# Turning three pairs of heads on TensorE, the second head's maxima row too, and a new table of the order

## The chip, the core and the metric

The kernel runs on one core of a Trainium2 chip. The metric is the device time of one execution in microseconds (us). The engines are named as the profile names them: PE (TensorE, matmul), DVE (VectorE), ACT (ScalarE), POOL (GpSimd) and SP (SyncE, which issues all DMAs of this kernel). PEld is PE's loading of weights, SPq is SP at issuing a DMA. Each engine works through its own instructions in the order in which they were written down; semaphores make it wait for others.

## The reference

An attention with pooled queries, then a mixer. Shapes: 4 batches, 8 heads, 1152 keys, 576 pooled queries, head width 64; 32 heads in all.

```python
def _attn_ref(q, k, v):
    q_pool = q.reshape(B, H, S // 2, 2, D).mean(axis=3)
    scores = scale * np.matmul(q_pool, k.transpose(0, 1, 3, 2))
    scores = scores - np.max(scores, axis=-1, keepdims=True)
    attn = np.exp(scores)
    attn = attn / (np.sum(attn, axis=-1, keepdims=True) + 1e-09)
    return np.matmul(attn, v)

def _moe_ref(x, w_tok1, w_tok2, w_ch1, w_ch2):     # x: (4, 576, 512)
    xt = x.transpose(0, 2, 1)
    u = x + (np.maximum(xt @ w_tok1, 0.0) @ w_tok2).transpose(0, 2, 1)
    return u + np.maximum(u @ w_ch1, 0.0) @ w_ch2
```

The weights arrive as 64-bit floats and are narrowed on the chip from their words.

## The kernel before, in words

**Numbers in two parts.** Each 32-bit operand of an important product is split into a high part, which PE takes in one pass, and a low part, what is left. A product is then two or three matmuls. For the scores a head has stacked operands: `KK` holds the keys' high part above their low part, `QQ` the queries' high part twice, and `K2`, `Q2` hold the rest of the product in 64 partitions. Partition 64 of `K2` is a row of -1, and partition 64 of `Q2` is the row of the queries' maxima, so that the score matmul itself subtracts the maximum (`scores` in `main`, L930 to L939: first `s<-qq,kk`, then `s<-q,k`). The row is needed before the second half of a head's first score.

**Heads come in pairs** (p = 0 to 15). `load_kq` (L665) loads keys and queries of two heads. For pair 0 the loads are wide: keys lie as they are in memory (`load_k`), queries with both members of a pool next to each other (`load_q`). PE turns these 128x128 blocks (`keys` L718, `queries` L747, steps L724 and L755). For all other pairs the loads are in blocks (`load_k_blocks` L674, `load_q_blocks` L680: twelve DMAs of runs of 128 bytes), laid so that DVE's transpose of 32x32 blocks completes the turn (L732, L764). The pooling addition is in `prep_kq` (L713 for pair 0, L707 for the others). ACT copies the high part out of PSUM, DVE subtracts it for the low part. `qd` holds the last 64 queries of both heads on a diagonal; ACT fills it for pair 0 (L778), two DMAs for the others (L782).

**`stack`** (L805) copies the parts by six DMAs per head into `QQ`, `KK`, `K2`, `Q2`.

**`maxima`** (L825) makes the raw scores of the high parts on PE (L871) and DVE reduces them (L873). From head 1 on, DVE reduces the three thirds of a query's keys to one column of `MH` (L838, L842), and four or five DMAs of single words turn the columns into the row of `Q2` (L846, L849). Head 0 goes another way (`first_maxima`, L882): DVE reduces into columns of `M0` (L893), PE turns them (L899), ACT copies the row (L906); the last 64 queries of head 1 come along there (L910).

**`main`** (L916) runs nine steps per head: scores of two key blocks, two exponentials on ACT (`pf` L951 in full, `ph` L954 the high part), their difference `pl` (L958; on POOL for the first four heads, on POOL or DVE after them), and the products with `v` (L985). **`finish`** (L1002) turns the result, forms denominators (L1041, L1044) and multiplies five blocks by the reciprocal on ACT (L1051). After each fourth head `token_mix` (L1055) mixes half of a batch over the tokens, with weights that `tok_weights` (L594) narrows early: ACT L638, POOL L640, DVE L644 to L655, ACT L653. Behind all heads the channel mixing runs (`mm3` L1214, `mm4` L1242).

**The order.** Nothing is issued as it is called. Each `step` adds an entry with an engine, an estimated cost and a due time (from the table `DUE`) to a plan, with its dependencies. `Plan.run` (L334) then issues them in an order that is read from the string `ORDER`, and gives the steps whose numbers stand in `OTHER` their second engine (`both` steps: POOL or DVE). Costs and due times served to make that table; `run` does not look at them:

```python
        near = np.frombuffer(zlib.decompress(base64.b85decode(ORDER)), np.uint8).reshape(2, -1)
        order = [self.steps[n] for n in np.cumsum(near.T.copy().view("<i2")[:, 0])]
        for n in OTHER:
            self.steps[n].eng, self.steps[n].cost = self.steps[n].other
```

Of the kernel before, what the change touches and what calls it, by code (L numbers as in the profile page):

```python
# [17 lines left out]
AF = mybir.ActivationFunctionType  # L18
# [19 lines left out]
    "scores": -2.93,  # L38
    "p_lo": 3.58,
    "sum": -9.57,  # L40
    "pv": 2.54,
    "o": -51.33,
    "finish": 8.58,
    "max": -33.49,
    "max_each": 0.15,
    "prep": -34.13,
    "v": 1.91,
    "stack": -25.67,
    "stack_2": -1.62,
    "mix": 3.46,  # L50
    "mix_x": 6.67,
    "w_tok": 25.38,
    "w_tok_each": 0.19,
    "w_bits": -16.65,
    "sum_each": 1.34,
    "pv_lo": -1.1,
    "lo_first": 24.87,
    "max_first": -16.17,
    "max_second": 26.42,
    "scores_each": -4.16,  # L60
    "p_hi": -0.36,
    "pv_one": -0.26,
    "finish_each": -13.78,
    "den_sum": -50.17,
    "x_lo": -20.89,
    "x": 46.21,
    "den": -101.88,
    "rd": -11.49,
    "u": 17.31,
    "u_each": -154.37,  # L70
    "max_of": -3.2,
    "max_row": -26.25,
    "max_first_each": -13.9,
    "q_pool": -8.21,
    "q_turn": 4.59,
    "k_each": 1.41,
    "k_hi": -501.55,
    "k_turn": -4.76,
    "q_diag": 2.44,
    "load_v_0": -10.17,  # L80
    "v_0": 20.76,
    "max_1": 24.7,
    "ut_load": 42.06,
    "k_lo": 1.85,
    "q_hi": -23.02,
    "q_lo": -22.23,
    "load_kq": -79.9,
    "load_v": -9.0,
    "v_lo": -23.38,
    "load_w_tok": -22.82,  # L90
    "mix_x_lo": -125.66,
    "mix_1": 1.01,
    "mix_t": -1.26,
    "mix_2": 3.21,
    "mix_u": -46.13,
    "w_ch": 7.79,
    "w_ch_each": 1.93,
    "ut_0": 13.85,
    "ut_1": -24.13,
# [7 lines left out]
class Due(dict):  # L107
# [16 lines left out]
    "TtF2szpK5X*m|`w4P8#;LPmT96=P&cKO6MnZeXr@N8hq0EUHY1D-5R|vDxAJ0&r<Nu9jSSJb-cvoP3M=#L%Kiiyku_o*8!!^bl&E79bf8tzc"
    "jtpuiR$8G$IbgcQ4mEe2|`;3=ajvl*yqdk4+KAi)y04jGo*4&rUrsOB%i6^z;iM=F-"
    "jK8$%N2f@@XF;ui@cTJ!gZgzTMc16r*Che43Y$HDRC;e%;2>iF1_L7jyv2cCF#$h%$^#IguGwMo^VxOFD=tyFxOTroMNbpzheMg0p*yZ|FNS"
    "XbH2TqTZ<Y&&a1+-"
    "e~aAG~Ajo>5NGF*`P_GaaOOqTDD*pIftSJwQ_f!?s=UH&Slx@YUY?KvYwkQxhvc7S+W!?{#?7GZjUx!Xx)#1VE>`w0mA_Yv%AqVj;<donByP"
    "4t94s`NJh&x_y(>cItAwrRhL9cB@j-wb=EgN1a6c>S5n*&-"
    "fvegT2lw;GML?ord@>eeXK>eb1y)JA>lZ^J85dZp}z;_sgoeD)dRg(i<htKJ_y7gQ0h7X6z159r7G}GidEmP$TaEzquC)QIW}jymH$?cZb{q"  # L130
    "KI;0yL!+)?m(Qhy`1ppFE2Lwl;g|C(3G5ucY2%y)p4qaR+#UGD5wo#X)72u^3+dC(`ShysynZJ6YpHiC@K5UU*}|sX_pNARD85GcM$+R$n|B"
    "qDhWB|R>3(5cPUniGkgWXhB$MG6dwyynIy{d1m9#!@QDiT0BjG{2tj}{!D$QqoHvN-"
    "j;76#9Ob(*3*21&@)5}v7cc$DJojkcZXYx@~Wk8n3aOmB!7ggfg>C!XCud$s+&<`>l8tC+MSKIQCgk{*QHf;^2-"
    "J5afXUBmltAAn^HCKG^iYLYzSt@In{UXp4&L8HTH~Y|cbgH;}hJTw)J$s~tAMQXJHg?kPu<@sjoStKc-"
    "k)?V=Ev_Eev}V_%01Wlrhy4LjV8Xg#(K>F>fqyW^wUbirobfgI_q+1+M{5=jY_MavYSKOH;7Jy;g6e)>gOL<toWTKQ4TBE8e)Ld^Y#H<QPOy"
    "$L;F|7d^&2pVRdZTd!LA)22lq*Mzp-jGLDBgMqyPZxgN7FBrL(uoTBQ@lh5MOW30?2HD9E6(D_GD&`aomA)hwKC?Cvz*Q>1km9cNTVp}E(AE"
    "B=D+*O|oUH<n*X7#qVOa8>K?Ji8owL+~PyRYA~H2lD5MW$$R`>PK&Ke991yWz8KMe?G=sPdieqo69U-"
    "^tF|+hvt|Kxf}Z{Lq$78+2P6gb}FpN>SwPD$#^3J)3W~Q$?rtNO2k&wqcjRrgn{3thrbrU$z!MFn9Q^&Tsd~UiQHo4dCwA##?wt!osF!8rQ;"
    "Z_Z&+dfVy0$QvJ`pIIoXzMn=V@x#Ok#e}5_MwJXhkf7A8HaG&M)8ue}T)1m-x_aA~OH<~O5s-"
    "7r6bg!74^4s3*y?D}L2U*`^Zl7mgt)G<Rx2JP;z!}?;g}Ie#t5K(?ob1vx?5Gr<nN?~zPF;U({xOReQOAikQ_j?fC5+DpqxVS_Xxr#7QERFz"  # L140
    "WY1&Zra&i{((_!*+3BePQ&tttyd)aCChnTe2Qwe|?%W&~m>N**a(l!Vb;oZVz(M0)jxfXanI-NVnK4zjYi0C$z7kCha4odmH#`(SHSc*%;;I"
# [36 lines left out]
    "$_0i8_I<z|Hcpsx;Y{xRRrP1buMsAX={GdHs4L#L(NcD;ce+i*DEy7HlxKapcIhi;T$wfESk!a#R%L%23_m^UYoF4$#%<4bQJO^K_1&TJZSN"
# [1174 lines left out]
```

## Time and profile before

| what | value |
|---|---|
| time, median of 3 runs | 893.98 us (892.14 to 895.11) |
| the profiled execution | 896.53 us, of it span 894.8 us |
| mean granted clock of PE | 0.981 of 2.4 GHz |
| PE busy | 850.1 us (95%), 5322 matmuls |
| PEld, DVE, ACT, POOL busy | 785.5, 625.6, 551.7, 478.0 us |
| attention and token mixing | up to about 580 us |
| channel mixing | about 580 us to the end |

How to read it: the profile is one execution. Busy times are unions of an engine's instructions. The records of matmuls overlap, so a busy PE need not be at its peak; the spacing of matmuls tells its pace. Waits are put down to what came last before an instruction began, by the events that the profile holds.

### The profile page before, as it was taken

The numbers are of one execution on the slowest core, as the hardware profiler recorded it, in microseconds if no ns is written. First come the engines' busy times: TensorE is split into PE (matmuls) and PEld (weight loads), VectorE is DVE, ScalarE is ACT, GpSimd is POOL, SyncE is SP. The second block draws the span as 40 slices with busy tenths as digits, with TensorE's granted clock in tenths as the row PEclk, the third lists the DMA queues.
The fourth block names the chain that finished last, engine by engine and source line by source line (L and its number), as shares of the span: only waits on it lengthen the run. The fifth ranks groups of instructions, "written<-read, shape, count | busy, mean of one in ns | idle before, by whom it ended". The sixth has DMA issues, their size and how long they took to land.

```text
span 894.8 us, 15517 instructions
## 1 busy us (share of the span) xinstructions
PE 850.1 (95%) x5322; PEld 785.5 (88%) x5322; DVE 625.6 (70%) x1244; ACT 551.7 (62%) x1141; POOL 478.0 (53%) x378
## 2 busy tenths in 40 slices
PE   7659989999999999999999999999999999999998
PEld 5549879999988899998999999999998999989897
DVE  5767989999999898988998988788774323121202
ACT  4758889798899689898799898843431211111110
POOL 2868978898997769788688777423210000000000
PEclk9959999999999999999999999999999999999999
DMA  7997786786796677687765563256533301000101
GB/s 172 150 192 149 140 151 115 141 167 123 137 177 113 128 148 134 134 174 145 135 139 114 110 135 89 68 154 170 141 97 70 71 7 41 1 30 1 46 2 36
DMA packets 262207, 99.46 MB, mean 111 GB/s; under 512 B 233264, under 2 KB 245424, under 8 KB 262128
## 3 DMA queue, kind: packets, MB, share of 16 engines
q1 hardware_dynamic: 262128, 98.47, 54.2%
q8 instruction: 42, 0.69, 0.3%
q14 instruction: 37, 0.30, 0.1%
HBM read 46.40 MB, written 9.44 MB: 62 GB/s over the span
## 4 chain that ended last, share of the span: by engine, by line
PE 70%; DVE 10%; DMA 6%; ACT 6%; SPq 5%; issue 2%; POOL 1%; DVEq 0%; ACTq 0%; POOLq 0%
PE r L1214 16%; PE o L985 13%; PE s L1242 12%; PE s L937 12%; PE r L871 6%; PE o L1242 4%; DVE sum L965 3%; DVE mx L873 3%; PE r L1100 2%; ACT ph L954 2%; ACT pf L951 2%; DMA vn<-in_v_dram 2%; PE r L1082 2%; SPq L682 2%; DMA q<-mh 2%
## 5 line engine op out<-in xcount | busy, mean ns | idle before, releaser
L958 POOL TENSOR_TENSOR pl<-pf,ph 128x576 fp32r<-128x576 f32 x247 | 355.4, 1461 | 80.2 <-ACT ph L954 24.9
L873 DVE TENSOR_REDUCE mx<-r 128x1 f32<-128x384 f32 x384 | 192.4, 548 | 27.2 <-PE r L871 24.1
L985 PE MATMUL o<-ph,vv 128*128 128x288 f32 (+2 forms) x882 | 205.8, 300 | 2.2 <-DVE ot L998 1.0
L951 ACT ACTIVATE pf<-s 128x576 f32<-128x576 f32 x288 | 191.4, 684 | 21.6 <-PE s L937 19.3
L954 ACT ACTIVATE ph<-s 128x576 fp32r<-128x576 f32 x288 | 187.8, 661 | 27.1 <-PE o L985 12.7
L937 PE MATMUL s<-qq,kk 128*128 128x288 f32 x574 | 175.1, 313 | 10.0 <-ACT ph L954 6.8
L937 PE MATMUL s<-q,k 65*128 65x288 f32 x576 | 169.7, 302 | 13.5 <-DMA qn<-in_q_dram 10.9
L985 PE MATMUL o<-pl,vv 128*65 128x288 f32 (+1 forms) x576 | 149.3, 300 | 0.3 <-POOL pl L958 0.3
L1222 DVE SCALAR_TENSOR_TENSOR h<-r,h 128x384 fp32r<-128x384 f32 x72 | 39.2, 554 | 156.3 <-ACT h L1220 156.2
L1220 ACT ACTIVATE h<-r 128x384 fp32r<-128x384 f32 x72 | 34.9, 491 | 182.5 <-PE r L1214 182.4
L985 PEld LDWEIGHTS o<-ph,vv 128*128 128x128 f32 (+2 forms) x882 | 128.9, 153 | 8.8 <-DVE ot L998 3.2
L937 PEld LDWEIGHTS s<-qq,kk 128*128 128x128 f32 x574 | 110.7, 193 | 20.5 <-ACT ph L954 11.3
L871 PE MATMUL r<-kk,qq 128*128 128x384 f32 x372 | 123.9, 349 | 3.5 <-DMA qq<-qh 1.9
L1242 PE MATMUL s<-w,h 128*128 128x512 f32 x468 | 124.7, 394 | 1.1 <-DVE raw L1256 1.1
L937 PEld LDWEIGHTS s<-q,k 65*128 65x128 f32 x576 | 111.3, 193 | 14.4 <-DMA qq<-qh 11.1
L1214 PE MATMUL r<-big,w 128*128 128x384 f32 x576 | 113.1, 337 | 0.6 <-DVE h L1222 0.4
L1214 PEld LDWEIGHTS r<-big,w 128*128 128x128 f32 x576 | 102.4, 188 | 6.7 <-DVE h L1222 0.6
L965 DVE TENSOR_REDUCE sum<-pf 128x96 f32<-128x960 f32 x90 | 100.7, 1133 | 0.6 <-ACT pf L951 0.6
L1242 PEld LDWEIGHTS s<-w,h 128*128 128x128 f32 x468 | 86.7, 188 | 15.2 <-DVE raw L1256 1.8
L985 PEld LDWEIGHTS o<-pl,vv 128*65 128x65 f32 (+1 forms) x576 | 90.1, 163 | 2.0 <-POOL pl L958 0.6
L871 PEld LDWEIGHTS r<-kk,qq 128*128 128x128 f32 x372 | 70.1, 192 | 8.6 <-issue 3.6
L1214 PE MATMUL r<-ut,w 128*128 128x384 f32 x288 | 58.5, 339 | 0.0
(133 smaller groups left out, 1121.9 us busy)
## 6 DMA issues: line engine op xcount, KB each, us to landing
raw<-in_moe_w_ch_dram SPq DMA_DIRECT2D x24, 512.0 KB, 3.8
vn<-in_v_dram SPq DMA_DIRECT2D x32, 288.0 KB, 3.9
kk<-kh SPq DMA_DIRECT2D x32, 288.0 KB, 3.4
kk<-kl SPq DMA_DIRECT2D x32, 288.0 KB, 4.2
qq<-qh SPq DMA_DIRECT2D x64, 144.0 KB, 3.3
k<-kk SPq DMA_DIRECT2D x31, 288.0 KB, 3.4
kn<-in_k_dram SPq DMA_DIRECT2D x60, 144.0 KB, 4.2
qn<-in_q_dram SPq DMA_DIRECT2D x120, 72.0 KB, 2.8
```

The costliest lines, as they stand in the source:

```text
L871: step(PE, mm(SP3), lambda ps=ps, w=w, x=x: te.matmul(at(ps)[:, 0:SP3], w, x, start=True, stop=True), t, read, [ps], [ps])
L873: step(DVE, dve(SP3), lambda ps=ps, m=m: ve.tensor_reduce(m, at(ps)[:, 0:SP3], axis=AX.X, op=ALU.max), t + due["max_of"], [ps], [key])
L937: te.matmul(at(st)[:, i, 0:HF], w[:, c * P:(c + 1) * P], x[:, fq * HF:(fq + 1) * HF], start=(n == 0), stop=(n == len(terms) - 1))
L951: step(ACT, act_ps(2 * HF) + (0 if near else 49), lambda pf=pf, st=st: sc.activation(pf, at(st)[:, :, 0:HF], AF.Exp, scale=ESC), t, [(st, ...
L954: step(ACT, act_ps(2 * HF) + 15, lambda ph=ph, st=st: sc.activation(at(ph), at(st)[:, :, 0:HF], AF.Exp, scale=ESC), t + due["p_hi"], [(st, ...
L958: both(2 * HF, lambda e, pf=pf, ph=ph, pl=pl: e.tensor_sub(at(pl), pf, f(at(ph))), t + due["p_lo"], [("pf", s), ph], [pl], [pl], on=POOL i ...
L965: step(DVE, 65 + 1.06 * (NK + 1) * HF // CUT, lambda fq=fq, cs=cs: ve.tensor_reduce(SUM[:, fq, cs], PF[:, 5 * fq:5 * fq + 5, cs].rearrange ...
L985: lambda o=o, x=x, w=w, m=m, i=i, c=c, new=new, end=end: te.matmul(at(o)[0:m - w], VV[i2][:, c, w:m], at(x)[:, i], start=new, stop=end),
L1214: te.matmul(at(ps)[:, 0:GT], w[:, c], x[:, c], start=(c == 0 and n == 0), stop=(c == NC4 - 1 and n == 2))
L1220: step(ACT, act_ps(GT), lambda: sc.activation(at(h)[:, 0], at(ps)[:, 0:GT], AF.Relu), t, [ps], [h])
L1222: step(DVE, dve(GT), lambda: ve.scalar_tensor_tensor(out=at(h)[:, 1], in0=at(ps)[:, 0:GT], scalar=0.0, in1=f(at(h))[:, 0], op0=ALU.max, op ...
L1242: te.matmul(at(ps), a[:, x * P:(x + 1) * P], w, start=(fi == 0 and m == 0), stop=(fi == NF - 1 and m == 2))
```

## The change

Pairs 0, 1 and 2 (`BY_PE = 3`) use the wide loads and PE's turns; pairs 1 and 2 have six loads each where they had twelve, and their `qd` is filled by ACT. Pair 3 is the first with block loads, and its query loads wait for all users of the query tile. The maxima of head 1 go head 0's way: `turn_rows`, taken out of `first_maxima`, is called for it with its four blocks of queries. The closing multiplies get DVE as a second engine. `ORDER`, `OTHER` (62 numbers before, 121 after) and `DUE` are new, and so are a dozen estimated costs. The diff without the tables and the estimates:

```diff
+    BY_PE = 3
@@ load_kq
+        gone = plan.users(("qn",))
@@ load_q_blocks
-                t, write=[("qn", j, y, x)], after=after, pieces=SQ)
+                t, write=[("qn", j, y, x)], after=gone if p == BY_PE else after, pieces=SQ)
...
         if p == 0:
             order = [(load_q, 0, 4), (load_k, 0, 3), (load_k, 3, NK), (load_q, 4, 5)]
+        elif p < BY_PE:
+            order = [(load_k, 0, NK), (load_q, 0, 4), (load_q, 4, 5)]
@@ prep_kq (and the same test in keys() and queries())
-        for i, (o0, o1) in enumerate(((0, 384), (384, SQ)) if p else ()):
+        for i, (o0, o1) in enumerate(((0, 384), (384, SQ)) if p >= BY_PE else ()):
...
-            if p == 0:
+            if p < BY_PE:
                 step(PE, 3 * TURN, turn, t + j * due["k_each"], read, [ps, ("kh", j), ("kl", j)], [ps])
             else:
...
-                    if p == 0:
+                    if p < BY_PE:
                         step(ACT, 230, lambda ps=ps, r=r, j=j, n=n: sc.copy(
-                            QD[0][r, j * REM:(j + 1) * REM], bank(ps)[r, n - REM:n]),
+                            QD[p % 2][r, j * REM:(j + 1) * REM], bank(ps)[r, n - REM:n]),
...
@@ maxima
         t += due["max_row"]
+        if h == 1:
+            turn_rows(1, [0, 1, 2, 3], t)
+            return
...
-        if h > 1:
-            step(DMA, 50, lambda: sy.dma_start(
+        step(DMA, 180, lambda: sy.dma_start(
...
@@ first_maxima
+        turn_rows(0, cs, t)
+
+    def turn_rows(h, cs, t):
+
         for c in cs:
-            m = MX[0][:, c] if c < 4 else RM
+            m = MX[h][:, c] if c < 4 else RM
...
             step(DVE, 72, lambda m=m, c=c: ve.tensor_reduce(
                 M0[:, D + c:D + c + 1], m, axis=AX.X, op=ALU.max), t, keys, [("m0", c)])
...
         step(ACT, act_ps(n), lambda: sc.copy(
-            Q2[0][D:D + 1, q0:q0 + n], at(ps)[D:D + 1, 0:n]), t, [ps],
-            [("row", 0, c) for c in cs])
+            Q2[h][D:D + 1, q0:q0 + n], at(ps)[D:D + 1, 0:n]), t, [ps],
+            [("row", h, c) for c in cs])
@@ finish
-            step(ACT, 200, lambda c=c, r=r, row=row: sc.mul(
-                u[r, row, col], turned()[r, c, 0:D], rd[r, c]),
-                t + due["u"] + due["u_each"] * (c > 3), [(ps, 0, c), ("rd", i2)], [out_, *stage])
+            step(ACT, 240, lambda e, c=c, r=r, row=row: (
+                e.mul(u[r, row, col], turned()[r, c, 0:D], rd[r, c]) if e is sc
+                else e.tensor_scalar(
+                    out=u[r, row, col], in0=turned()[r, c, 0:D], scalar1=rd[r, c], scalar2=None, op0=ALU.mult)),
+                t + due["u"] + due["u_each"] * (c > 3), [(ps, 0, c), ("rd", i2)], [out_, *stage],
+                other=(DVE, 140))
@@ issue
-            s.fn(*([(ve, po)[s.eng == POOL]] if s.other else []))
+            s.fn(*([{ACT: sc, DVE: ve, POOL: po}[s.eng]] if s.other else []))
```

## Rows read from the trace of the kernel before

**Rows 1.** Page, part 2: busy tenths of PE and its granted clock in 40 slices.
```profile
PE   7659989999999999999999999999999999999998
PEclk9959999999999999999999999999999999999999
```

**Rows 2.** Stretches: us, busy PE, PEld, DVE, ACT, POOL (x instructions), clock, DMA share, GB/s.
```profile
31.10:38.50 7.40, 5.73 (x44) 4.92 (x41) 5.19 (x12) 4.75 (x12) 5.67 (x5) 1.00 0.97 206
38.50:49.70 11.20, 0.33 (x5) 0.14 (x2) 7.09 (x20) 4.83 (x15) 7.01 (x8) 0.67 0.94 157
49.70:66.50 16.80, 11.77 (x38) 9.48 (x39) 13.19 (x31) 10.72 (x24) 12.70 (x11) 0.51 0.97 191
130.00:580.00 450.00, 438.31 (x3146) 416.66 (x3144) 402.79 (x800) 394.47 (x821) 361.80 (x277) 0.99 0.67 131
```

**Rows 3.** Waits of PE from 20 to 75 us: total, times, longest.
```profile
PE s L937 <- DMA qn<-in_q_dram: 10.9, 1, 10.9
```

**Rows 4.** Timeline, 31 to 50 us: start, duration, engine, line, operation.
```profile
32.06 0.15 DVE L838 TENSOR_REDUCE mh<-mx 128x4 f32<-128x12 f32 x1
36.78 4.30 SPq L682 DMA_DIRECT2D qn<-in_q_dram  x8
38.44 0.38 PE L937 MATMUL s<-qq,kk 128*128 128x288 f32 x1
41.13 0.52 SPq L846 DMA_DIRECT2D q<-mh  x1
49.69 0.58 PE L937 MATMUL s<-q,k 65*128 65x288 f32 x1 [10.87 <-DMA qn<-in_q_dram]
```

**Rows 5.** Lines of maxima row (38 to 50 us) and query load, ns.
```profile
DMA to landing us min/median/max: 2.3/5.5/6.3
L682 SPq DMA_DIRECT2D qn<-in_q_dram x37: 312/564/1970, 21.1 to 99.6; - x37
```

**Rows 6.** Timeline, pair 0's turns, head 0's row and its copy.
```profile
9.31 0.82 PE L724 MATMUL r<-ident,kn 128*128 128x128 f32 x6
18.66 0.49 PE L899 MATMUL r<-ident,m 128*65 128x128 f32 x3
19.18 0.47 ACT L906 CAST q<-r 1x384 fp32r<-1x384 f32 x1 [6.82 <-PE r L899]
```

**Rows 7.** Chain of work, 20 to 130 us: start, duration, what.
```profile
29.14 1.98 DMA qn<-in_q_dram
63.52 0.48 PE s L937 x2
78.02 0.53 PE s L937 x4
```

**Rows 8.** DVE by line and shape, 0 to 210 us: busy, mean ns.
```profile
L732 DVE STREAM_TRANSPOSE r<-kn 128x384 f32<-128x384 f32 x16 | 8.9, 576 | 0.0
L764 DVE STREAM_TRANSPOSE r<-qp 128x192 f32<-128x192 f32 x6 | 2.3, 380 | 0.1
```

**Rows 9.** Lines of the closing multiply and the diagonal copy, ns min/median/max.
```profile
L1051 ACT ACTIVATE u<-r,rd x160: 284/313/388, 39.6 to 578.4; 128x64 f32<-128x64 f32 x128, 64x64 f32<-64x64 f32 x32
L778 ACT CAST qd<-r x2: 206/206/207, 10.9 to 11.1; 64x64 fp32r<-64x64 f32 x2
```

**Rows 10.** Waits of PE from 100 to 140 us.
```profile
PE r L871 <- DMA qq<-qh: 1.9, 1, 1.9
PE s L937 <- DMA q<-mh: 1.1, 1, 1.1
```

**Rows 11.** Timeline, first closing step of heads 1, 2 and 3 on DVE.
```profile
83.44 0.15 DVE L1041 TENSOR_SCALAR den<-r 128x5 f32<-128x5 f32 x1
103.65 0.15 DVE L1041 TENSOR_SCALAR den<-r 128x5 f32<-128x5 f32 x1
117.62 0.16 DVE L1041 TENSOR_SCALAR den<-r 128x5 f32<-128x5 f32 x1
```

**Rows 12.** POOL by line and shape, 20 to 130 us: busy, mean ns.
```profile
L958 POOL TENSOR_TENSOR pl<-pf,ph 128x576 fp32r<-128x576 f32 x46 | 65.4, 1443 | 15.7 <-ACT pf L951 9.3 <-ACT ph L954 2.4 <-PE o L985 2.0
```

More of the change, by code (lines that the diff above doesn't have):

```diff
@@ L37 @@
 DUE = {
[L38 to L99, printed above, removed]
+    "scores": -2.92,
+    "p_lo": 3.46,
+    "sum": -10.49,
+    "pv": 2.51,
+    "o": -70.24,
+    "finish": 8.09,
+    "max": -33.39,
+    "max_each": -0.28,
@@ new lines @@
+    "prep": -33.13,
+    "v": 4.68,
+    "stack": -30.16,
+    "stack_2": 2.5,
+    "mix": 3.42,
+    "mix_x": 6.69,
+    "w_tok": 3.87,
+    "w_tok_each": 1.27,
+    "w_bits": 2.23,
+    "sum_each": 1.4,
+    "pv_lo": -1.08,
+    "lo_first": -7.13,
+    "max_first": -7.31,
+    "max_second": 5.49,
+    "scores_each": -5.66,
+    "p_hi": -0.24,
+    "pv_one": -0.21,
+    "finish_each": -8.96,
+    "den_sum": -31.57,
+    "x_lo": 10.49,
+    "x": 1.09,
+    "den": -4328.6,
+    "rd": -39.41,
+    "u": 17.12,
@@ new lines @@
+    "u_each": -51.59,
+    "max_of": -1.39,
+    "max_row": -109.74,
+    "max_first_each": 54.31,
+    "q_pool": -4.49,
+    "q_turn": 2.43,
+    "k_each": 3.89,
+    "k_hi": -49.76,
+    "k_turn": -6.59,
+    "q_diag": -5.9,
+    "load_v_0": -1.46,
+    "v_0": 13.99,
+    "max_1": 1.63,
+    "ut_load": 31.17,
+    "k_lo": -705.19,
+    "q_hi": -35.41,
+    "q_lo": -29.35,
+    "load_kq": -15.19,
+    "load_v": -4.55,
+    "v_lo": -48.7,
+    "load_w_tok": 22.92,
+    "mix_x_lo": -27.91,
+    "mix_1": -0.15,
@@ L100 @@
+    "mix_t": -0.78,
+    "mix_2": 2.59,
+    "mix_u": -91.85,
+    "w_ch": 2.79,
+    "w_ch_each": 110.93,
+    "ut_0": 42.85,
+    "ut_1": -14.73,
     "stay": 800,
@@ L124 @@
[L124 to L129, printed above, removed]
@@ L264 @@
+OTHER = (20, 214, 434, 435, 436, 437, 445, 473, 620, 621, 632, 768, 769, 934, 1007, 1161, 1256,
[7 rows of a table added]
 class Buf:
@@ L795, in prep_v @@
         vn, vv = VN, VV[h % 2]
-        step(DMA, 1.3 * wire(4 * S * D),
+        step(DMA, 1.7 * wire(4 * S * D),
              lambda: sy.dma_start(vn, v[h // H, h % H].rearrange("(c p) d -> p c d", p=P)),
@@ L799, in prep_v @@
         hi, lo = (slice(x, x + D) for x in ((D, 0) if h in IN_PV else (0, D)))
-        step(ACT, act(NK * D), lambda: sc.copy(vv[:, :, hi], vn),
+        step(ACT, act(NK * D) + 50, lambda: sc.copy(vv[:, :, hi], vn),
              t, ["vn"], [("vv", h % 2)])
@@ L812, in stack @@
                 (1, KK, KLO, S, [("kl", x) for x in range(3)])):
-            step(DMA, (1.3 if dst is QQ else 1.8) * wire(4 * D * n),
+            step(DMA, (1.58 if dst is QQ else 1.7) * wire(4 * D * n),
                  lambda half=half, dst=dst, src=src: sy.dma_start(
@@ L889, in first_maxima @@
                 t += due["max_first_each"]
+        turn_rows(0, cs, t)
+    def turn_rows(h, cs, t):
         for c in cs:
-            m = MX[0][:, c] if c < 4 else RM
-            keys = [("mx", 0, c, n) if c < 4 else ("rm", n) for n in range(3)]
+            m = MX[h][:, c] if c < 4 else RM
+            keys = [("mx", h, c, n) if c < 4 else ("rm", n) for n in range(3)]
             step(DVE, 72, lambda m=m, c=c: ve.tensor_reduce(
@@ L995, in main @@
                         continue
-                    step(ACT, 420, lambda o=o, qs=qs: sc.copy(
+                    step(ACT, 540, lambda o=o, qs=qs: sc.copy(
                         LOW[:, qs], at(o)[D:P]), t + due["o"], parts, [("low", fq)])
@@ L1066, in token_mix @@
             r = rows(c)
-            step(ACT, act(CM), lambda r=r, c=c, x=x: sc.copy(XH[r, c], x[r, cols]),
+            step(ACT, act(CM) + 45, lambda r=r, c=c, x=x: sc.copy(XH[r, c], x[r, cols]),
                  t, keys(c), [("xh", c)])
@@ L1160, in load @@
                         "(c p) f -> p c f", p=P))
-        step(DMA, wire(8 * P * C), load, t - 3, ["first"], [raw], [raw], pieces=4 * P)
+        step(DMA, 1.2 * wire(8 * P * C), load, t - 3, ["first"], [raw], [raw], pieces=4 * P)
         for n, (eng, cost, fn) in enumerate(narrow(lambda: at(w), lambda: at(raw), C)):
```

298 lines of the change are left out of this document (153 added, 145 removed), and 10 rows, old and new, of the table OTHER.

## The prediction

> **What bounds the kernel now.** I read the page's strips first [rows 1]. TensorE (PE) is at nine tenths in 35 of 40 slices. The weak ones are the first three, up to 67 us, and the granted clock falls in the third. So the change, which touches the first pairs of heads, works where PE has something to lose; between 130 and 580 us PE is busy 438.31 of 450 us [rows 2]. A busy PE is not a PE at its peak, so idle time and spacing are used below, not busy shares.
>
> The table of stretches [rows 2] then finds the hole: between 38.5 and 49.7 us PE is busy 0.33 us in five instructions. The clock is already lower there (mean 0.67), and from 49.7 to 66.5 us it is 0.51, practically the lower level of 1.2 GHz, though PE works again. The wait list shows one wait of 10.9 us [rows 3]. It names a load of `qn`, only because that landed last; the instruction that waits is `s<-q,k`, the second half of head 1's first score, which reads no `qn`. Its `q` tile carries in partition 64 the row of head 1's maxima. The timeline [rows 4] tells this row's story: the maxima are reduced at 32.06 us, but the four DMAs that lay them out as a row stand in SyncE's (SP's) queue behind eight `qn` loads (36.78 us, 4.30 us long). They are issued from 41.13 us on, and these rows take 2.3 to 6.3 us to land [rows 5]. PE's last work before is the first half of that score, at 38.44 us; the second starts at 49.69 us. So head 1 waits 17 us for data that lie on the chip, and PE stands idle for 10.9 us of it.
>
> **The change, part by part.**
>
> What costs nothing: the numbers in `DUE` and the estimated costs in `step(...)` are read only when steps are made; `run()` takes the order from `ORDER` and the engine from `OTHER`. They change no instruction. What acts is the order, the engines, `BY_PE = 3`, `turn_rows` and its `h == 1`.
>
> *Row of head 1 by PE.* Four DVE reductions, each taken at the 0.15 us of the one that they replace [rows 4] (+0.45 us), come first, then four PE turns and one ScalarE (ACT) copy. Head 0 did the same with three turns that span 0.49 us and a copy of 0.47 us [rows 6]; with a fourth turn this is about 0.45 + 0.6 + 0.5 = 1.6 us, and allowing as much again for the hops the row is there at about 32.1 + 3 = 35 us, before PE is done with head 0. Four DMAs leave SP's queue. The wait of 10.9 us goes: **-10.9**. The ends: 0, if the order puts the turn late, and -12.6, if head 1's scores also fill what PE idles between 31.1 and 38.5 us (7.4 - 5.73 = 1.7 us).
>
> *The low clock behind the hole.* It fell after PE had stood idle. Between 49.7 and 66.5 us PE issues 38 matmuls; two scores take 0.48 us there and four take 0.53 us later [rows 7], that is 240 against 133 ns. So 38 x 0.107 = 4.1 us of PE time come back. PE also waits there for ACT's exponentials (busy 11.77 of 16.8 us), so not all of it counts: **-3**, with ends 0 and -4.1.
>
> *Pairs 1 and 2 turned by PE.* Per pair, three DVE turns of 0.576 us for the keys, one as wide for the queries, and one of 0.380 us go [rows 8]: 2.7 us, for both 5.4 us of DVE. PE gets 14 turns per pair. Six of pair 0's span 0.82 us [rows 6], at most 0.14 us each; 28 turns are 3.8 us, and 4.4 us with the row's four. Pair 1's fall between 20 and 40 us, where PE has gaps of its own; pair 2's fall among work that PE waits for. **+2**, with ends 0 and +4.4.
> Here a rule speaks against the change: the Trainium skill, "VectorE: DVE Perf Modes", section "The three transpose paths", gives 390 ns for a 128x128 transpose on TensorE and 311 ns on VectorE (bf16). By that price PE would pay 28 x 0.39 = 10.9 us, and the sum would come out some 7 us later, at an estimated 887 us. The trace disagrees: 0.14 us for a turn on PE.
>
> *Loads and SP's queue.* A wide pair takes six loads instead of twelve. The block loads cost SP about 0.56 us each [rows 5], so two pairs free 12 x 0.56 = 6.7 us of SP. The `qd` copies go from DMA to ACT (four DMAs less, 2.3 us; ACT pays 4 x 0.21 us [rows 9]), and with the row 20 issues or some 11 us leave the queue, all of them in the first 120 us. Of PE's waits between 100 and 140 us, 1.9 and 1.1 us end at `qq` and row DMAs that stood in that queue [rows 10]. **-2**, with ends 0 and -3. Pair 3's query loads now wait for all readers of pair 2's queries (`gone`); the blocks they overwrite already waited for both additions, so I take 0, and +1 if the one small last addition is late.
>
> *Closing multiplies.* `OTHER` grows, and entries that are runs of neighbours (434 to 437, 3633 to 3637, 5074 to 5078) look like the closing multiplies of a head; I count about 35 of 160. On ACT one takes 0.31 us [rows 9]; 35 are 11 us off ACT over 540 us and, at an estimated 0.15 to 0.38 us, between the rows of DVE's small reduction and of its 192-column turn [rows 4, 8], 5 to 13 us onto DVE, about what the turns took off it. Between 130 and 580 us DVE is busy 402.79 and ACT 394.47 of 450 us [rows 2], and a shift of some 10 us leaves both below PE: **0**, with ends -2 and +2.
>
> *The new order behind 130 us.* PE is idle 450 - 438.31 = 11.7 us there [rows 2]. A new order can win or lose some of it, and nothing in the profile says which: **0**, with ends -5 and +5.
>
> Sum: -10.9 - 3 + 2 - 2 + 0 + 0 = -13.9 us. The profiled execution took 896.53 us (span 894.8 us); 13.9 less is 882.6 us. The median of the runs shown is 893.98, 2.5 us below that execution, so the forecast is **880 us**, with 875 to 887 as its own range.
>
> **Rivals.**
> 1. *More comes back.* From 49.7 to 66.5 us the clock itself may set the pace. Then half of the 16.8 us, 8.4 instead of 3, returns. Also head 1 may close up: it closes at 83.44 us, 33.8 us after its first score, and heads 2 and 3 follow it by 20.2 and 14.0 us [rows 11]. At 20.2 us head 1 would give 13.6 us on top of the hole. With the other terms at 0 the sum is -10.9 - 8.4 = -19 to -10.9 - 13.6 = -24.5, so 875 down to 869; with SP's 2 us and half an order's gain the low end is 866. I name **871 us**. For it: the twenty issues freed in SP. Against it: GpSimd (POOL), next.
> The first half of this is what the Trainium skill, "TensorE: Matmul & The Clock Gate", section "HAM oscillation — how this bites in real kernels", reckons: a stretch at the low clock loses half its length. The wait of PE on ACT in that stretch speaks against the full half.
> 2. *The hole was not empty.* While PE stood, DVE worked 7.09, ACT 4.83 and POOL 7.01 us of 11.2 us [rows 2], on the token weights. That work must now go beside heads 1 to 3. POOL is pinned there (`on=POOL` for the first four heads): a head's nine subtractions are 9 x 1.443 = 13.0 us [rows 12], before weights and queries. If POOL becomes the bound, the 7 us return: -13.9 + 7 = -6.9, **887 us**, and up to 894 if the order also lets the row come late, so that the change doesn't do what it says.
> 3. *Slower.* DVE's turns waited in DVE's queue; the new ones stand in PE's, which is served in order, ahead of scores and products that are ready. Eleven groups are added (five per pair and the row). Before the first turn of pair 1 the chain of work waits 1.98 us for a load [rows 7]. If each group stands 1.9 us, that is 21 us: 880 + 21 = **901 us**. It is slower than before from 13.9 / 11 = 1.3 us per group on. For it: the loads of both pairs share SP with the stacks of heads 1 to 3. Against it: half as many loads stand ahead of each turn.
>
> **How the numbers follow.** The forecast gets 0.48, rival 1 0.22, rival 2 0.17, rival 3 0.13. From 866 to 892 us leaves out rival 3 (0.13), the far end of rival 1 and of rival 2 (some 0.06). A measurement of this kernel tells about 0.3% from no change, 2.7 us: faster is below 891.3, slower above 896.7 us. Faster: 0.48 + 0.22 + most of rival 2 = 0.79; same: the rest of rival 2 and of 3's near end, 0.09; slower 0.12.
>
> **What would show it.** Right: no PE wait above 3 us between 30 and 60 us; head 1's first score before 40 us; the clock at 1.00 from there on; head 1's closing 10 to 25 us earlier than 83.44 us, and from there to the end the same distance as before. PE's turns of pairs 1 and 2 with waits below 1 us. Wrong: a new hole before head 2 or 3 with POOL or a stack DMA at its end; many waits at the turns' line; or a gain up to 130 us that is given back later, which would say that another engine, and not the head start, sets the attention's pace.

## The result and the profile after

The kernel after takes 886.4 us (median) where the kernel before takes 893.4 us on the same chip: ratio 0.9915 (95% interval 0.9889 to 0.994), 7 us or 0.85% faster. One of the four executions of the kernel after took 1017.81 us at a mean granted clock of 0.75, and the ratio leaves it out. The forecast was 880 us, so the sign and the range held and the size was about half. The profiled execution took 886.56 us, of it span 884.8; that of before had lain 2.5 us above its median, which is why the two traces differ by 10 us and the medians by 7.

Page, part 2, answers to [rows 1] (busy tenths of PE, granted clock, 40 slices):

```profile
PE   8889999999999999999999999999999999999998
PEclk9979999999999999999999999999999999999999
```

The stretches of [rows 2] (us, busy PE, PEld, DVE, ACT, POOL, clock, DMA share, GB/s):

```profile
38.50:49.70 11.20, 7.72 (x37) 5.51 (x35) 9.43 (x24) 9.95 (x23) 11.03 (x10) 0.75 1.06 254
49.70:66.50 16.80, 15.27 (x91) 13.13 (x92) 16.27 (x39) 8.85 (x22) 14.17 (x13) 0.86 0.65 119
130.00:580.00 450.00, 435.59 (x3124) 411.45 (x3123) 403.78 (x840) 378.62 (x757) 352.37 (x272) 1.00 0.68 133
```

The hole is gone: 37 matmuls stand between 38.5 and 49.7 us where five stood. But PE is not full there. It is busy 7.72 of 11.2 us, and DVE, ACT and POOL are now nearly full. From 130 to 580 us PE's busy time is much as before (435.59 against 438.31 us).

Three lines of the wait list of PE from 20 to 75 us (in us: total, times, longest), against the 10.9 us of [rows 3]:

```profile
PE s L954 <- ACT ph L971: 2.5, 4, 1.3
PE o L1002 <- POOL vv L814: 1.6, 1, 1.6
...
PE r L766 <- DVE kl L754: 0.5, 1, 0.5
```

No wait is longer than 1.6 us, and the turns' line (L766) waits 0.5 us. The timeline shows what became of [rows 4], the row of head 1's maxima: four PE turns, ACT's copy, and the two halves of head 1's first score.

```profile
27.39 0.73 PE L916 MATMUL r<-ident,m 128*65 128x128 f32 x4
28.70 0.58 ACT L923 CAST q<-r 1x512 fp32r<-1x512 f32 x1
...
35.01 0.30 PE L954 MATMUL s<-qq,kk 128*128 128x288 f32 x1
35.15 0.29 PE L954 MATMUL s<-q,k 65*128 65x288 f32 x1
```

The row is there at 29.3 us and head 1's first score begins at 35.01 us (38.44 before). Its second half, which reads the row, follows 0.14 us behind the first; before, it followed 11.25 us behind.

The first closing steps of heads 1, 2, 3 (compare [rows 11]) and of the last head:

```profile
72.72 0.15 DVE L1058 TENSOR_SCALAR den<-r 128x5 f32<-128x5 f32 x1
97.60 0.14 DVE L1058 TENSOR_SCALAR den<-r 128x5 f32<-128x5 f32 x1
109.98 0.17 DVE L1058 TENSOR_SCALAR den<-r 128x5 f32<-128x5 f32 x1
...
565.62 0.16 DVE L1058 TENSOR_SCALAR den<-r 128x5 f32<-128x5 f32 x1 [0.21 <-PE r L1039]
```

and of the last head in the kernel before:

```profile
575.08 0.15 DVE L1041 TENSOR_SCALAR den<-r 128x5 f32<-128x5 f32 x1
```

Head 1 closes 10.7 us earlier than before, head 2 6.1, head 3 7.6 and the last head 9.5 us; the spans differ by 10.0 us. What is won by 130 us is kept to the end about one for one. Head 0 closes later, at 49.43 us instead of 38.67: in the new order heads 0 and 1 run side by side, so that part of the work that fills the hole is head 0's.

So far this looks like the forecast: the wait named in it is gone, and some 10 us of trace time with it. The experiments ask which part did that. All ratios are against the kernel before on the same chip. Lines shift from kernel to kernel, so the lines of a step differ between the fences below; the tiles name it. Where an edit adds or drops steps, `ORDER` and `OTHER` follow: a new step stands where the one stood that it replaces, or ahead of its first reader, and the others keep their order. No such order was made anew.

### The profile page after: what moved, and what is told of

Read it like the earlier page. It is cut to its first block, busy times and chain, and to the rows that moved or that the text cites. A ratio compares the mean times of both kernels' runs of the same rounds, so it can differ in the third digit from the quotient of the medians.

```text
span 884.8 us, 15490 instructions
## 1 busy us (share of the span) xinstructions
PE 852.8 (96%) x5354; PEld 783.3 (89%) x5354; DVE 629.9 (71%) x1296; ACT 541.9 (61%) x1089; POOL 472.5 (53%) x378
## 4 chain that ended last, share of the span: by engine, by line
PE 74%; DVE 11%; DMA 5%; ACT 4%; SPq 3%; issue 2%; POOL 1%; DVEq 0%; ACTq 0%
PE r L1234 17%; PE o L1002 14%; PE s L1262 12%; PE s L954 11%; PE r L884 7%; DVE mx L886 4%; PE o L1262 4%; PE r L1102 2%; DVE sum L982 2%; PE r L1120 2%; DMA kk<-kl 2%; ACT ph L971 1%; DMA kk<-kh 1%; PE r L1039 1%; ACT pf L968 1%
## 5 line engine op out<-in xcount | busy, mean ns | idle before, releaser
L1002 PE MATMUL o<-ph,vv 128*64 128x288 f32 (+2 forms) x882 | 204.5, 301 | 4.0 <-DVE ot L1015 1.6
L971 ACT ACTIVATE ph<-s 128x576 fp32r<-128x576 f32 x288 | 185.3, 656 | 25.6 <-PE o L1002 11.8
L954 PE MATMUL s<-qq,kk 128*128 128x288 f32 x574 | 172.8, 310 | 4.8 <-ACT ph L971 3.7
L954 PE MATMUL s<-q,k 65*128 65x288 f32 x576 | 166.9, 299 | 0.3 <-DMA q<-mh 0.2
L1002 PEld LDWEIGHTS o<-ph,vv 128*64 128x64 f32 (+2 forms) x882 | 128.3, 153 | 9.8 <-DVE ot L1015 2.9
L1262 PE MATMUL s<-w,h 128*128 128x512 f32 x468 | 122.6, 393 | 0.8 <-DVE raw L1276 0.8
L1234 PE MATMUL r<-big,w 128*128 128x384 f32 x576 | 111.2, 336 | 0.0
L1188 POOL TENSOR_TENSOR w<-v,w 128x512 fp32r<-128x512 f32 x16 | 21.3, 1332 | 96.1 <-ACT w L1187 88.8
```

Of the source, the lines that this page charges most:

```text
L954: te.matmul(at(st)[:, i, 0:HF], w[:, c * P:(c + 1) * P], x[:, fq * HF:(fq + 1) * HF], start=(n == 0), stop=(n == len(terms) - 1))
L971: step(ACT, act_ps(2 * HF) + 15, lambda ph=ph, st=st: sc.activation(at(ph), at(st)[:, :, 0:HF], AF.Exp, scale=ESC), t + due["p_hi"], [(st, ...
L1002: lambda o=o, x=x, w=w, m=m, i=i, c=c, new=new, end=end: te.matmul(at(o)[0:m - w], VV[i2][:, c, w:m], at(x)[:, i], start=new, stop=end),
L1234: te.matmul(at(ps)[:, 0:GT], w[:, c], x[:, c], start=(c == 0 and n == 0), stop=(c == NC4 - 1 and n == 2))
L1262: te.matmul(at(ps), a[:, x * P:(x + 1) * P], w, start=(fi == 0 and m == 0), stop=(fi == NF - 1 and m == 2))
```

## Experiments around the row and the token weights

In the kernel after, DVE and POOL are well filled from 38.5 to 66.5 us and ACT to 49.7 us, the narrowing of the token weights among their work, and PE idles in pieces. Rival 2 of the prediction named POOL as the bound. Two kernels ask POOL and DVE.

**a_noclip** drops POOL's nine clips of the token weights.

```diff
-                step(POOL, 150 + 3.3 * m, lambda tmp=tmp: po.tensor_scalar(
-                    out=tmp(), in0=tmp(), scalar1=F64_LEAST, scalar2=F64_MOST,
-                    op0=ALU.max, op1=ALU.min), t, [w], [w])
+                step(POOL, 150 + 3.3 * m, lambda: None, t, [w], [w])
```

> The changed kernel without the nine POOL instructions that clip the token weights (L648, 1.05 to 1.17 us each, 10 us in all); everything else stands in the same order. The clipping, and only that, is left out. Theory (POOL took the place of the row's wait): POOL works without a pause from 34.1 to 61 us in the changed kernel, and 10 us of that are the clips; without them heads 0 and 1 close 6 to 10 us earlier and the time falls to 877 to 881 us. Rival (the stack of head 2 sets the pace: its copies of kk land 5.6 us after issue, and head 2 cannot start earlier): head 0 closes earlier, but head 2 does not, and the time stays within 2 us of 886. Rival (the rest of the forecast went into the order behind 130 us): the same, 886.

**a_clipdve** gives the same clips to DVE, in the same places.

```diff
-                step(POOL, 150 + 3.3 * m, lambda tmp=tmp: po.tensor_scalar(
+                step(POOL, 150 + 3.3 * m, lambda tmp=tmp: ve.tensor_scalar(
```

> The changed kernel with the nine clips on DVE in place of POOL, in the same place of the order; nothing is left out. Theory (POOL binds from 34 to 61 us): POOL loses 10 us, DVE gets nine of some 0.3 us, 2.7 us, and DVE is itself busy 25.7 of the 28 us from 38.5 to 66.5; so part comes back: 880 to 884 us. Rival (all engines are equally full there): what POOL loses DVE adds, 886 to 888. Rival (stack DMAs bind): 886.

Busy times from 40 to 60 us (same columns as the stretches above) in a_noclip, a_clipdve and the kernel after:

```profile
40.00:60.00 20.00, 16.74 (x74) 13.47 (x75) 18.63 (x46) 13.29 (x31) 12.80 (x11) 0.66 0.96 192
```

```profile
40.00:60.00 20.00, 14.47 (x54) 10.91 (x55) 18.92 (x48) 13.38 (x32) 8.68 (x8) 0.54 0.80 173
```

```profile
40.00:60.00 20.00, 15.18 (x71) 11.44 (x72) 18.47 (x46) 13.18 (x31) 19.83 (x19) 0.74 0.83 175
```

Without the clips POOL falls from 19.83 to 12.80 us, DVE stays at 18.6, and the time does not move: ratio 0.9907 (0.9888 to 0.9926), head 1 at 72.18 instead of 72.72 us. POOL, though full, bounds nothing here that shows in the time, though PE's granted clock is lower too in this trace, 0.66 against 0.74. With the clips on DVE, head 1 closes at 77.78 and the last head at 570.31 us, each some 5 us later than in the kernel after. The ratio, 0.9938 (0.992 to 0.9955), overlaps that of the kernel after, and the profiled execution lies 2.4 us above its median, so the 5 us rest on one trace. Nor are they the price of DVE work alone. The nine clips take 6.2 us on DVE: six of them 0.28 to 0.58 us, three 1.2 to 1.5 us. The three lie beside POOL's subtractions `pl`, as the first two here; the clock is lower as well, 0.54 from 40 to 60 us.

```profile
34.65 4.25 POOL L975 TENSOR_TENSOR pl<-pf,ph 128x576 fp32r<-128x576 f32 x3 [1.89 <-ACT ph L971]
36.07 2.98 DVE L648 TENSOR_SCALAR w<-w 128x256 f32<-128x256 f32 x2
```

What bounds in POOL's place is not shown by these two kernels. The rival that the stack of head 2 sets the pace expected the same time of a_noclip; in its trace and in that of the kernel after no engine waits for a DMA from 30 to 75 us, which speaks against it. DVE, busy 18.5 to 18.9 of 20 us in all three, and ACT are what is left; b_rowpe and a_defer, below, bear on them.

**a_rowdma** is the kernel after with head 1's row laid out by four DMAs again, put where the reductions for the turn had stood.

```diff
-        if h == 1:
-            turn_rows(1, [0, 1, 2, 3], t)
-            return
...
```

> The changed kernel, but with head 1's row again laid out by four DMAs, issued right behind the reduction; the rest of the change stays. Theory: the row lands some 6 us later (four issues of 0.6 us and up to 5 us to land) and head 1's scores start that much later, but POOL is the bound from 34 us on, so that the loss is 3 to 6 us: 889 to 892. Rival (the row alone is what the change brings): the whole gain goes, 893 to 896. Rival (wide loads had already emptied SP's queue, so that a row by DMA is early enough): 886 to 888.

Its ratio is 0.9895 (0.9875 to 0.9916): no slower than the kernel after. Head 1 closes at 72.35 us (72.72 there). The timeline says why (start, duration, engine, line):

```profile
27.27 0.17 DVE L812 TENSOR_REDUCE mh<-mx 128x4 f32<-128x12 f32 x1
27.46 2.47 SPq L820 DMA_DIRECT2D q<-mh  x4
30.04 1.88 SPq L662 DMA_DIRECT2D qn<-in_q_dram  x3
```

The four DMAs are issued 0.2 us behind the reduction, ahead of `qn` loads; before, they were issued 9 us behind it, after eight of them [rows 4]. What made the row late was a place in SP's queue. With the place mended, the PE turn has nothing left to save in this order.

**b_rowpe** is the opposite: the kernel before, in its own order, with only the row of head 1 by PE.

```diff
         t += due["max_row"]
+        if h == 1:
+            turn_rows(1, [0, 1, 2, 3], t)
+            return
...
```

> The kernel before, with head 1's row turned by PE in the place of its reduction and nothing else changed; the order of all other steps is that of before. Forecast's step (the wait of 10.9 us goes, -10.9, and -3 for the clock): 880 to 884. Theory (the hole was not empty: the exponentials and subtractions of head 1 stand in ACT's and POOL's queues behind the token weights, whose loads land at 48.8 us): little comes back, 889 to 893. Rival (the row's part is nothing): 893 to 894.

It should have brought 10.9 us and brought 0.2%: ratio 0.9982 (0.9964 to 1.0001). The row lies ready at 33.1 us, where before PE had it at 49.69 us [rows 4]. The wait list of PE from 20 to 75 us (first line) and the timeline:

```profile
PE s L914 <- ACT pf L928: 8.4, 2, 8.2
```

```profile
32.49 0.58 ACT L883 CAST q<-r 1x512 fp32r<-1x512 f32 x1 [1.22 <-PE r L876]
40.81 0.38 PE L914 MATMUL s<-qq,kk 128*128 128x288 f32 x1
...
46.08 0.37 ACT L623 CAST big<-r 128x256 fp32r<-128x256 f32 x1 [0.62 <-DVE r L620]
...
48.36 0.48 ACT L742 CAST qh<-r 128x384 fp32r<-128x384 f32 x1 [0.97 <-DVE r L734]
48.74 0.66 ACT L931 ACTIVATE ph<-s 128x576 fp32r<-128x576 f32 x1
49.63 0.65 ACT L928 ACTIVATE pf<-s 128x576 f32<-128x576 f32 x1
```

PE now makes head 1's first scores from 40.81 us on, fills the two score buffers and waits 8.2 us for an exponential. The first one starts at 48.74 us. Ahead of it in ACT's queue stand, among others, three casts of the token weights (L623), each of which waits 0.3 to 0.6 us for DVE's step (L620), and a cast of `qh`, which waits 0.97 us for DVE's turn (L734). A wait for a DMA was replaced by a wait for work that had filled the hole.

If the token weights are in the way there, they might be moved. **a_defer** and **b_rowpe_defer** spread their 64 compute steps over later places, from head 1's scores to behind head 3's, in the order of the kernel after and of b_rowpe. Only the string changes: in the kernel after the nine chains stand at places 255 to 419 of 6860, in a_defer one chain begins about every 60 to 80 places, from 380 to 960 (b_rowpe_defer the same from 400).

```diff
-ORDER = (
...
+ORDER = (
...
```

> The kernel after with the same spreading of the token weights. Theory W: the pieces of 1 us in which PE idles between 38 and 55 us close up, the clock stays at 1.00, heads 1 to 3 close 3 to 6 us earlier: 880 to 883 us, better than both kernels. Rival S (DVE is as full beside heads 2 and 3): 885 to 888 us, with head 1 earlier and head 3 not.

> The kernel before with the row of head 1 by PE, as in b_rowpe, and with the 63 steps that narrow the token weights spread from head 1 to behind head 3's scores instead of in one block between heads 0 and 1. Theory W (the token weights in ACT's and DVE's queues took the place of the row's wait): the wait of PE on head 1's first exponential, 8.2 us in b_rowpe, shrinks below 3 us, head 1 closes near 72 us instead of 81.8, and 5 to 8 us of the forecast 10.9 come out at the end: 885 to 888 us. Rival S (the same 15 us of DVE work only moves beside heads 1 to 3, where DVE is full as well): head 1 closes early, head 3 as late as in b_rowpe, 892 to 894 us.

Both are the slowest kernels of all, 1.0198 (1.0171 to 1.0224) and 1.0217 (1.0195 to 1.024), and no theory had expected a loss of such a size. PE's waits in a_defer from 15 to 130 us, and the stretches in which DVE runs dry:

```profile
PE r L854 <- DVE w2l L633: 6.1, 2, 3.8
PE r L854 <- DVE mx L856: 4.1, 9, 1.5
```

```profile
35.00:40.00 5.00, 4.25 (x33) 3.96 (x32) 0.17 (x2) 4.18 (x8) 3.38 (x4) 1.00 0.59 177
40.00:45.00 5.00, 3.59 (x26) 2.80 (x24) 0.35 (x2) 3.89 (x8) 3.51 (x3) 1.00 1.11 249
```

A chain keeps one of the three PSUM banks `r` from its first DVE step to its last (L633), and the raw scores (L854) take their banks from the same three. Beside the maxima of heads 2 to 4 PE waits for the bank. Meanwhile DVE stands idle where the chains were taken out (busy 0.17 and 0.35 of 5 us). Of the places tried, the block between heads 0 and 1 is the best. How far the bank, DVE's queue and the clock (0.88 from 20 to 130 us against 0.95 in the kernel after) make the 23 us is not told apart.

## Experiments on the pairs, `qd` and the multiplies

**b_bype** is the kernel before, in its own order, with pairs 1 and 2 by wide loads, PE's turns and ACT's `qd` copies; **b_both** has the row of head 1 by PE as well. That is all of the change but the new order and the multiplies.

```diff
+    BY_PE = 3
...
-            if p == 0:
+            if p < BY_PE:
                 step(PE, 3 * TURN, turn, t + j * due["k_each"], read, [ps, ("kh", j), ("kl", j)], [ps])
...
-                    if p == 0:
+                    if p < BY_PE:
...
```

> The kernel before, in its own order, with the wide loads and PE's turns for pairs 1 and 2 (BY_PE = 3), the row of head 1 still by DMAs. Theory D: DVE and SP's queue are relieved in front of head 1, whose row was held up behind eight query loads; the row lands earlier and the hole of 10.9 us gets shorter by 3 to 6 us: 887 to 890 us. Rival H (the hole is set by the token weights as the run with the row by PE alone showed, and the turns were off the path): 892 to 894 us.

> The kernel before, in its own order, with all parts of the change but the new order and the closing multiplies: row of head 1 by PE, wide loads, PE's turns and ACT's qd copies for pairs 1 and 2. Theory T (the parts work only together with an order made for them: the token weights still stand in ACT's and DVE's queues ahead of head 1's exponentials, and PE's turns wait for a bank that they hold): 890 to 895 us, as with each part alone. Rival C (each part alone left the other's wait, both together close the hole): 880 to 886 us.

Neither is faster: 1.0023 (1.0002 to 1.0045) and 1.0005 (0.9989 to 1.0022). The wait list of PE in b_both from 15 to 130 us, first line, and the place in the timeline:

```profile
PE r L728 <- DVE big L625: 6.5, 1, 6.5
```

```profile
44.30 1.81 POOL L686 TENSOR_TENSOR qp<-qn 64x128 f32<-64x128 f32 x3
45.80 0.75 DVE L625 TENSOR_TENSOR big<-r,big 128x256 fp32r<-128x256 f32 x2
46.33 0.50 PEld L728 LDWEIGHTS r<-ident,qp 128*128 128x128 f32 x3 [6.59 <-POOL qp L686]
46.36 0.87 PE L728 MATMUL r<-ident,qp 128*128 128x128 f32 x3 [6.48 <-DVE big L625]
46.88 0.59 PE L917 MATMUL s<-qq,kk 128*128 128x288 f32 x1
```

Here PE stands in its own queue at the turn of pair 2's pooled queries (L728), and head 1's first score waits behind it until 46.88 us. The turn lacks two things that come within 0.2 us of each other: the queries' additions on POOL (L686), which stand behind clips of token weights, and a bank that a token-weight chain frees with L625. It is the mechanism of rival 3, with one stall of 6.5 us in place of eleven of 1.9 us, and once more the token weights stand where the hole was. The stall belongs to the place as well: PE's turn stands where DVE's stood in the order of before.

**a_block** goes the other way: the kernel after, in its own order, with block loads, DVE's turns and `qd` by DMA for pairs 1 and 2.

```diff
-    BY_PE = 3
+    BY_PE = 1
...
```

> The kernel after, in its own order, but pairs 1 and 2 by block loads and DVE's turns again (BY_PE = 1). Eight turns, 2.7 us of DVE for each pair, come back, PE loses 28 turns, SP gets 16 DMAs more. Theory D (DVE's queue is late from 38 to 60 us, so what is taken off it there comes forward one for one): heads 1 to 3 close 3 to 6 us later than in the kernel after, and the time is 889 to 892 us. Rival O (the new order and the closing multiplies brought the gain, the turns nothing): closings within 1 us, 885.5 to 887.5 us. Rival P (PE's turns cost what I forecast, 2 us): 884 to 885 us.

It is much slower than any of the theories allowed, 1.0094 (1.0073 to 1.0115), and slower than before. The timeline shows a new hole ahead of head 2's first raw score, which reads `qd`:

```profile
32.82 5.10 SPq L654 DMA_DIRECT2D qn<-in_q_dram  x8
...
33.83 0.33 ACT L746 CAST qh<-r 128x192 fp32r<-128x192 f32 x1
...
38.57 1.18 SPq L756 DMA_DIRECT2D qd<-qh  x2
41.11 0.66 PE L847 MATMUL r<-kh,qd 128*128 128x384 f32 x1 [6.37 <-DMA qd<-qh]
```

`qh` is there at 34.2 us, but the two copies to the diagonal come behind eight query loads of pair 2 (5.1 us) in SP's queue, and PE waits 6.37 us. The two copies stand there because this order has the cast of `qh` that they read behind these loads; no run moved the loads. Two kernels split the 14 us between `qd` and the loads with their turns.

**a_qd_dma** is the kernel after with only `qd` of pairs 1 and 2 by DMA.

```diff
-                    if p < BY_PE:
+                    if p == 0:
                         step(ACT, 230, lambda ps=ps, r=r, j=j, n=n: sc.copy(
                             QD[p % 2][r, j * REM:(j + 1) * REM], bank(ps)[r, n - REM:n]),
...
```

> The kernel after with one thing undone: the last 64 queries of pairs 1 and 2 (qd) are laid on their diagonal by two DMAs for each pair, as before, and not by ACT; wide loads and PE's turns stay. Theory Q (in a_block, 14 us slower than the kernel after, PE stood 6.4 us at a raw score that reads qd, because the two DMAs were issued 4.7 us after qh was there, behind nine query loads in SP's queue): the same wait, shorter since pair 2's loads are six and not twelve: 3 to 6 us, 889 to 893 us. Rival L (the block loads and DVE's turns made a_block slow, qd nothing): 885.5 to 888 us.

**a_block_qdact** is a_block with `qd` by ACT.

> The kernel after with block loads and DVE's turns for pairs 1 and 2, as in a_block, but qd filled by ACT as in the kernel after. Theory Q: the wait of 6.4 us and PE's idle 2.3 us ahead of it go, 7 to 10 of a_block's 14.3 us come back: 890 to 894 us. Rival L: nothing comes back, 898 to 901 us. What is left above 886.4 us is the price of block loads with DVE's turns.

a_qd_dma: 890.3 us, 0.9973 (0.9959 to 0.9988), with one wait on `qd` where theory Q had it:

```profile
PE r L854 <- DMA qd<-qh: 4.0, 1, 4.0
```

a_block_qdact: 894.42 us, 1.0013 (0.9999 to 1.0026). Its timeline, and that of the kernel after, for pair 1's loads, turns and last `qh`:

```profile
26.22 2.40 SPq L654 DMA_DIRECT2D qn<-in_q_dram  x4
29.61 1.05 DVE L706 STREAM_TRANSPOSE r<-kn 128x384 f32<-128x384 f32 x2 [1.82 <-DMA qn<-in_q_dram]
35.50 0.31 ACT L746 CAST qh<-r 128x192 fp32r<-128x192 f32 x1
```

```profile
20.90 2.25 SPq L699 DMA_DIRECT2D qn<-in_q_dram  x2
27.95 0.82 PE L735 MATMUL r<-ident,kn 128*128 128x128 f32 x6
30.43 0.90 PE L766 MATMUL r<-ident,qp 128*128 128x128 f32 x5 [0.53 <-DVE kl L754]
32.88 0.31 ACT L783 CAST qh<-r 128x192 fp32r<-128x192 f32 x1
```

With twelve loads SP issues until 28.6 us, with six until 23.2; the pair is ready 2.6 us later. By medians (the kernel before had 893.3 to 893.4 us beside each), undoing the `qd` copies costs 3.9 us, undoing loads and turns 8.0 us, and both together 14.3 us, in the new order only. The 3.9 us are the wait of 4.0 us. The 2.6 us are not the 8.0: in a_block_qdact head 1 closes at 77.46 us, 4.7 later than in the kernel after, head 6 9.4 and the last head 8.0 us later, and the granted clock from 20 to 130 us is 0.89 against 0.95. What the clock has in it is not told apart.

**a_act_u** puts the 57 closing multiplies that the kernel after has on DVE back on ACT.

```diff
-OTHER = (20, 214, 434, 435, 436, 437, 445, 473, 620, 621, 632, 768, 769, 934, 1007, 1161, 1256,
...
+OTHER = (20, 445, 473, 632, 934, 1007, 1161, 1256, 1485, 1491, 1650, 1673, 1978, 3063, 3402, 3849, 3877, 3912, 3923,
...
```

> The kernel after with all 160 closing multiplies on ACT; 57 of them were on DVE at 0.28 us, they take 0.31 us on ACT. 16 us go off DVE and 18 us onto ACT over 540 us, ends as they were in the order. Theory 0 (both engines are below PE, so the split is worth nothing): 885 to 888 us. Rival A (ACT's exponentials are what PE waits for most in the kernel after, and a multiply ahead of one in ACT's queue holds PE): 2 to 6 us slower, 888.5 to 892 us.

888.78 us, 0.996 (0.9943 to 0.9977), against 0.9915 (0.9889 to 0.994): some 2 to 4 us are lost. PE's waits on the multiply from 130 to 580 us, in a_act_u and in the kernel after:

```profile
PE r L1032 <- ACT u L1062: 2.9, 6, 0.7
PE r L877 <- ACT u L1062: 1.3, 5, 0.3
```

```profile
PE r L884 <- ACT u L1069: 0.7, 2, 0.3
PE r L1039 <- ACT u L1069: 0.2, 1, 0.2
```

PE waits 4.2 us there for the bank that ACT's multiply reads, instead of 0.9 us for ACT's and 0.4 us for DVE's. By this trace what counts is when the bank comes free, not the load of an engine: ACT and DVE are both below PE in that stretch.

## Why the prediction was right or wrong, point by point

That 886.4 us lies in the range of 875 to 887 us is in good part luck: the largest term of the sum, the row, is worth nothing by itself, and terms that were forecast at 0 together carry the gain.

- **The row of head 1, -10.9: wrong.** The wait was read rightly, its price was not. It went away in b_rowpe, and 0.2% came back (the interval reaches from 0.4% to nothing), since 8.2 us of a wait for ACT took its place; in the new order the same row by DMA costs nothing (a_rowdma). The step that failed is the one behind it: "The wait of 10.9 us goes", at its full length, without working out what stands next in ACT's queue. Rival 2 had it ("The hole was not empty") at 0.17 and named the wrong engine: in the kernel after POOL could be relieved of 7 us for nothing, and in b_rowpe PE's wait ran through the queues of ACT and DVE.
- **The low clock, -3: the sign held, not the level.** "The clock at 1.00 from there on" failed: it is 0.75 and 0.86 in the two stretches, against 0.67 and 0.51; by these means an estimated 10 of the 28 us lie at the lower level, against 24 before. From 40 to 60 us PE is busy in pieces, 15.18 of 20 us, with the clock at 0.74. Five microseconds at a time:

```profile
40.00:45.00 5.00, 3.11 (x15) 2.19 (x15) 4.14 (x11) 4.72 (x11) 4.83 (x6) 0.90 1.10 265
45.00:50.00 5.00, 3.30 (x14) 2.30 (x12) 4.50 (x12) 4.04 (x10) 5.00 (x5) 0.50 1.01 225
```

  No wait here is longer than 1.6 us, and still the clock is at its lower level (0.50, that is 1.2 GHz) from 45 to 50 us, after PE had been idle 1.9 of the 5 us before, in short pieces. In these rows the clock falls behind PE's gaps, and no run changes it alone. It is part of every price above: from 20 to 130 us it is 0.95 in the kernel after, 0.89 before, 0.91 in a_clipdve, 0.89 in a_block_qdact and 0.84 in a_block. So the reckoning of the Trainium skill, "TensorE: Matmul & The Clock Gate", section "HAM oscillation — how this bites in real kernels", that a stretch at the low clock loses half its length, was neither shown nor refuted.
- **Pairs by PE, +2: not measured by itself in the old order, sign wrong in the new one.** b_bype has this term and the next in one, forecast at 0 together, and is 2 us slower (1.0002 to 1.0045). In the new order, loads and turns together are worth -8.0 us, with the clock in it. I counted the DVE turns as off the path and PE's as on it, and gave nothing for when the pair is ready, 2.6 us earlier for pair 1. "0.14 us for a turn on PE" held: six span 0.82 us in the kernel after. The rule cited from the Trainium skill, "VectorE: DVE Perf Modes", section "The three transpose paths", which would have made the turns dear, does not fit: it gives 390 ns for one (bf16).
- **Loads and SP's queue, -2: direction right in the new order, size too small.** The ACT copies of `qd`, a clause of that paragraph, are worth 3.9 us by themselves. I priced the issue slots; the price is the wait of the one instruction that stands behind them, 4.0 us in a_qd_dma.
- **Closing multiplies, 0: off by some 2 to 4 us, and counted wrongly.** 57 of 160 are on DVE, not 35; one takes 0.28 us there (0.15 to 0.38 was estimated). PE waits 1.3 us for their bank instead of 4.2.
- **New order, 0 behind 130 us: right there; ahead of it it had no term.** The order by itself is no gain: with block loads, DVE's turns and `qd` by DMA it is 0.9% slower than before, the row by PE and the multiplies on DVE included (a_block). And the parts without it are no gain either (b_both, 1.0005). So the 7 us are seen only with parts and order together. But the new order was made for the new parts, and no order was made anew for the old ones: whether they could have won the same with one stays open.
- **Rivals.** Rival 1 (0.22) did not come. Rival 2's mechanism took the row's term, and its time, 887 us, is the nearest of all, but by another engine. Rival 3's stall is real where the order is not made for the turns (6.5 us in b_both).
- **What would show it.** No PE wait above 3 us, a first score of head 1 at 35.01 us, closing 10.7 us earlier, about the same distance to the end, short waits at the turns: all as written. Only the clock was not. In a_rowdma, where DMAs lay out the row, head 1 closes at 72.35 us and no wait is longer than 1.6 us either, so these signs told the two theories apart less than I thought. The sum came out at half of the forecast 13.9 us, and none of the terms that were tested by themselves had its forecast size in both orders.

## What to carry to other kernels

A long wait of one engine is not a price: before taking it at full length, follow each in-order queue past the waiting instruction and ask what the next consumer stands behind; here the row by PE uncovered a wait of 8.2 us for ACT, and row and turns together one of 6.5 us. Where the order of issue is written out, test an edit and its order apart and together, since parts that cost 14 us when undone in the order made for them were worth nothing in another. And when a small DMA feeds the bottleneck, price its place in the queue, not its issue.

## What the runs showed that was not expected

A full engine need not bound: POOL was busy 19.83 of 20 us, and taking 7 us off it changed nothing. The three PSUM banks `r` did bound, off and on: token-weight chains, turns, raw scores and closings share them, and PE's waits in a_defer (3.8 us at once) and a_act_u (4.2 us in all) were for a bank that another engine had not yet read. PE's clock fell to its lower level with no idle above 1.6 us in the wait list. And three clips on DVE took 1.2 to 1.5 us beside POOL's subtractions, where six took 0.28 to 0.58 us; why is not shown.
